# Decoding step of two layers: where the last 64 rows of w3 and wq lie in SBUF

## The chip, the cores and the metric

The kernel runs on one core of a Trainium2 chip. A core has five engines with instruction streams of their own: TensorE (PE; its weight loads are shown as PEld), VectorE (DVE), ScalarE (ACT), GpSimd (POOL) and SyncE (SP). Sixteen DMA engines move data between memory (HBM) and SBUF, which has 128 partitions. The metric is the device time of one execution in microseconds; lower is better.

## The reference

Two layers, each an attention block over a long cache and a mixer block, for one token of two sequences (D = 576, 32 heads, 16384 cached keys of 128, F = 4608).

```python
def _A_ref(x, k_cache, v_cache, wq, wo):
    q = (x @ wq).reshape(B, Sq, H, Dh).transpose(0, 2, 1, 3)
    scores = jnp.einsum("bhqd,bhkd->bhqk", q, k_cache) * (Dh ** -0.5)
    p = _softmax(scores, axis=-1)
    o = jnp.einsum("bhqk,bhkd->bhqd", p, v_cache)
    return o.transpose(0, 2, 1, 3).reshape(B, Sq, H * Dh) @ wo

def _B_ref(x, w1, w2, w3, w4):
    h = _gelu(_layernorm(x, axis=-1) @ w1)
    ...
    x1 = x + hs
    h2 = _gelu(_layernorm(x1, axis=-1) @ w3) @ w4
    return x1 + h2

x = x + _A_ref(_layernorm(x, axis=-1), A_k_cache, A_v_cache, A_wq, A_wo)
x = x + _B_ref(_layernorm(x, axis=-1), B_w1, B_w2, B_w3, B_w4)
```

The last two lines run twice, with the same weights and the same cache. With one token per sequence the four shifted parts of the mixer are zero, so `hs` is a constant. Both layers read the whole K and V caches, 64 tiles of 4 MB each (32 heads of 2 sequences), and all of wq, wo, w3 and w4.

## The kernel before

**Stages.** A layer is `q_projection`, `attention`, `rows_projection` of wo, `z_projection` (w3), GELU, and `rows_projection` of w4; `layer` (L645) lists them. The kernel records every operation in a graph (`Graph`), which puts semaphores between engines; the order of the recording is the order on each engine.

**Memory.** All cache tiles and weights go through one buffer `mem` of six slots of 32 KB a partition (`TILE`). `Store` hands it out: `plan` (L278) queues transfers in a fixed order, `pump` (L286) issues the first of the queue as soon as its place is free, and stops at the first that is not; `release` gives a place back when PE has read it and pumps again. All transfers are issued by SP, in the order of the queue. A plan entry has a list of starts, each a DMA of its own.

**The seam between the layers.** At the end of layer 0's attention two cache tiles stay in their slots for layer 1, and the K chunks of a third are kept. Between them lies a ring of six places of 4608 bytes a partition: four in slot 4 (`a`) and two in slot 1 (`c`), in the turn of L522. wo, w3 and w4 of layer 0 and wq of layer 1 go through it, place after place; `halves` (L525) cuts each block of 128 rows of w3 or wq into two halves of the columns. Behind them come the four quarters of a parked V tile (places 1, 2, 3 and 0 of `a`) and the first quarter of the first fresh K tile (in `c`), in the order of L539; then whole tiles again. In the seam PE also transposes K chunks of the kept tiles (`turn`, L1060) between the weights' matmuls.

**The end.** In layer 1 the weights lie in slots that the last tiles have left: wo in three pieces, w3 as whole blocks of 128 rows with all columns, w4 in six pieces, then w1. L550 to L557 give their places.

**The tail.** D = 576 is four blocks of 128 rows and a tail of 64. In `x` and its normalised form `xn` the 64 tail features lie on partitions 64 to 127 of the fifth block (`TL` = 64). Before, `plan_cols` (L440) loads a tail of w3 or wq with one DMA that splits each row into two halves, so that row r lies on partitions 2r and 2r + 1 and all 128 partitions are filled. To match, `spread_tail` (L719) multiplies the tail features with two selection matrices `sel`, and copies the result as `xt`: two column pairs, each with the features on every second partition and zeros between. `cols_tail` (L759) then needs half as many matmuls as there are column blocks, each with four columns: one pair for the first half of the columns, one for the second. `cols_chunk` (L740) does the full blocks, with one matmul for each 128 columns.

Of the kernel before, what the change touches and what calls it, by code (L numbers as in the profile page):

```python
# [328 lines left out]
class KB:  # L329
# [11 lines left out]
    PARKED = 5  # L341
    GONE = 72
    RAW = 2
    TURNS = {("w3", 0): 1, ("w3", 1): 1, ("w3", 2): 1, ("w4", 1): 1, ("w4", 3): 1, ("w4", 6): 1, ("w4", 8): 1,
             ("wq", 0): 1, ("wq", 1): 1, ("wq", 2): 1}

# [25 lines left out]
    def _alloc(self):  # L372
# [20 lines left out]
        self.spread = self.prod[:, 10 * U:14 * U]  # L393
        self.otn = self.prod[:, 14 * U:15 * U]
        self.fold = sb("fold", [128, 32], BF16)
        self.gT = self.prod[:, 4 * MT * B:5 * MT * B]
        self.z = self.prod[:, 512:512 + 2 * MT * B].bitcast(FP32)
        self.rows = self.prod[:, 1024:1024 + self.D]
# [41 lines left out]
    def plan_cols(self, nm, l, w, parts):  # L440

        self.parts[nm, l] = parts
        for i, (k, m, z, at) in enumerate(parts):
            n = 128 * (z - m)
            if k < self.KT - 1:
                src = w[k * 128:(k + 1) * 128, 128 * m:128 * z]
            else:
                n //= 2
                src = w[k * 128:, :].rearrange("r (h n) -> (r h) n", h=2)
            self.store.plan((nm, l, i), f"{nm}{k}_{m}", at, 2 * n, [(lambda b: b, src)])  # L450

    def whole(self, w, ats):

# [45 lines left out]
    def plan_all(self):  # L499
# [12 lines left out]
        for (t, u), slot in zip(tiles, place):  # L512
# [9 lines left out]
        turn = iter([*a, c[0]] + [a[0], a[1], c[1], a[2], a[3], c[0]] * 6)  # L522
        h = MT // 2
        self.cuts["wo", 0] = [(i, i + 4, next(turn)) for i in range(0, 32, 4)]
        halves = lambda n: [(k, m, z, next(turn)) for k in range(self.KT - 1) for m, z in ((0, n), (n, 2 * n))] + \  # L525
                           [(self.KT - 1, 0, 2 * n, next(turn))]
        w3 = halves(h)
        self.groups = [(0, 4, 8, 12, 16, 18), (0, 8, 12, 16, 18)]
        g = self.groups[0]
# [6 lines left out]
        b, hh = third % self.B, third // self.B  # L536
        tiles = self.tile_order(1)
        b2, h2 = tiles[0][1] % self.B, tiles[0][1] // self.B
        for i in (1, 2, 3, None, 0):  # L539
            if i is None:  # L540
                self.plan_piece(*tiles[0], T, self.K[b2, h2].rearrange("(p j) d -> p (j d)", p=128), 0, quarter)
            else:
                self.plan_piece("v", third, 4 * T, self.V[b, hh].rearrange("(p j) d -> p (j d)", p=128),
                                i * self.GONE // 4, self.GONE // 4)
        place = [(3, 4, 5, 0, 2, 1)[i % 6] for i in range(len(tiles))]
        for i, (t, u) in enumerate(tiles):
            if (t, u) != ("v", third):
                self.plan_tile(t, u, place[i], (quarter, half, half + quarter) if i == 0 else
                               (half,) if i == len(tiles) - 1 else (), 0 if i else quarter)
        self.cuts["wo", 1] = [(0, 11, 2 * T), (11, 22, 2 * T + 11 * row), (22, 32, 0)]  # L550
        at = 10 * row
        w4_at = T + 2 * w3r + w3r // 2
        self.cuts["w4", 1] = [(0, 8, w4_at)] + \
                             [(a, b, 3 * T + (a - 8) * row) for a, b in ((8, 16), (16, 26), (26, 30), (30, 34), (34, 36))]
        self.plan_rows("wo", 1, self.wo, self.cuts["wo", 1])
        self.plan_cols("w3", 1, self.w3, self.whole(self.w3, [at, at + w3r, T, T + w3r, T + 2 * w3r]))
# [88 lines left out]
    def layer(self, l):  # L645
        if l == 0:
            self.unscaled()
        self.q_projection(l)
        if l == 0:
            self.hs_projection()  # L650
            self.quads()
        self.attention(l)
        ot = self.otn.rearrange("p (b j) -> p j b", b=self.B)
        self.rows_projection("wo", l, lambda k: ot[:, k, :], "prod")
        self.add_psum(self.x, "x", self.x, "x", self.unscaled)
        self.layernorm("x", self.x, self.xb, "xb")
        self.dv(lambda e: e.tensor_copy(out=self.mean0[:, :], in_=self.mv[:, 0, :]), reads=["mv"], writes=["mean0"])
        self.dv(lambda e: e.tensor_copy(out=self.rstd0[:, :], in_=self.rstd[:, :]), reads=["rstd"], writes=["rstd0"])
        self.dv(lambda e: e.tensor_tensor(out=self.x1[:, :, :], in0=self.xb[:, :, :], in1=self.hs[:, :, :],
                                          op=ALU.add), reads=["xb", "hs"], writes=["x1"])  # L660
        self.z_projection(l)
        if l == 0:
            self.turn(2, settle=False)
        self.gelu_z()
        self.settle()
        self.rows_projection("w4", l, lambda k: self.gT[:, k * self.B:(k + 1) * self.B], "prod")
        self.dv(lambda e: e.tensor_tensor(out=self.x[:, :, :], in0=self.x[:, :, :], in1=self.x1[:, :, :],
                                          op=ALU.add), reads=["x", "x1"], writes=["x"])
        if l < self.NL - 1:
            self.add_psum(self.x, "x", self.x, "x", self.unscaled)  # L670
        else:
            self.add_psum(self.xo, "xo", self.x, "x")


    def quads(self):

# [39 lines left out]
                                          in1=self.rstd[TL:, :], op=ALU.mult),  # L716
                reads=["tmp1", "rstd"], writes=[dk])

    def spread_tail(self):  # L719

        B, KT = self.B, self.KT

        def f(pe):
            for h in range(2):
# [15 lines left out]
    def cols_chunk(self, w, l, k, out, pk, n, rhs, rk, cols, first, last=False, held=False):  # L740
# [15 lines left out]
        if l == (1 if w == "wq" else 0):  # L756
            self.turn(self.TURNS.get((w, k), 0), settle=not held)

    def cols_tail(self, w, l, out, pk, n, cols):  # L759

        B, k = self.B, self.KT - 1
        nm = (w, l, len(self.parts[w, l]) - 1)
        buf = self.store.buf(nm)

# [29 lines left out]
    def q_projection(self, l):  # L794
# [13 lines left out]
        for k in range(1, KT - 1):  # L808
            self.cols_chunk("wq", l, k, out, [pk], n, self.xn[:, k, :], "xn", cols, k == 1)
            if k == 1:  # L810
                self.spread_tail()
        self.cols_tail("wq", l, out, [pk], n, cols)
        self.act(lambda e: e.activation(out=self.junk[:, :], in_=self.eps[:, :], func=ACT.Exp),
                 reads=["eps"], writes=["junk"])
# [71 lines left out]
    def z_projection(self, l):  # L886
# [8 lines left out]
        self.layernorm("x1", self.x1, self.xn, "xn", after=lambda: chunk(1))  # L895
        if l == 0:
            self.settle()
        self.spread_tail()
        al, be = self.coef[:, 0, :], self.coef[:, 1, :]
        self.dv(lambda e: e.tensor_tensor(out=be, in0=self.mean0[:, :], in1=self.rstd0[:, :], op=ALU.mult),  # L900
                reads=["mean0", "rstd0"], writes=["coef"])
# [555 lines left out]
```

## Time and profile before

| what | value |
|---|---|
| median of 3 runs | 2550.74 us (2550.16 to 2550.76) |
| the profiled execution's own time | 2549.84 us |
| its span, first to last instruction | 2548.1 us |
| bytes moved | 1093.19 MB, mean 429 GB/s over the span |
| busy share PE, DVE, ACT | 63%, 74%, 47% |
| mean granted TensorE clock | 0.574 |

A core's profile is read in this order: the busy shares say which engine could bound the span; the row of slices says where in time the rates change; the chain of waits, followed back from the last instruction, says what ended last at each step. A share is an average over stages with different limits, so the stage around the change is read by itself. In tables by stretches a DMA share can be a little over 1, where packets of an engine overlap. The profile numbers no DMA engine.

### The profile page before, as it was taken

The page shows a single profiled execution, that of the slowest core. Times are in us where ns is not written, and L with a number is a line of the kernel's source. Part 1 is how long each engine was busy: PE and PEld are TensorE (multiplying, and loading weights), DVE is VectorE, ACT ScalarE, POOL GpSimd, SP SyncE. Part 2 cuts the span into 40 slices and gives each one's busy share as a digit, 9 for nine tenths or more (in the row PEclk, how much of TensorE's full clock was granted, in tenths as well). Part 3 has the DMA queues.
Part 4 walks back from the last instruction along what each step waited for, and adds up shares of the span by engine and source line. Part 5 has one row for each costly group of instructions (what it writes and reads, how often), then busy time and mean ns, then how long its engine had stood idle before and what let it go on. Part 6 is the DMA issues. An engine that isn't in the chain of part 4 may idle for free.

```text
span 2548.1 us, 74893 instructions
## 1 busy us (share of the span) xinstructions
PE 1614.7 (63%) x34407; PEld 1580.7 (62%) x34407; DVE 1897.0 (74%) x2062; ACT 1204.2 (47%) x1810; POOL 53.5 (2%) x151
## 2 busy tenths in 40 slices
PE   4666666656666666666777766656665666666566
PEld 3666666656666665666667666656665665666566
DVE  5877777777777777777648877777777777777774
ACT  3544544444454444445435544444454444445442
POOL 0000000000000000000000000000000000000000
PEclk8555555555555555555656555565555555555555
DMA  9999999999999999999999999999999999999999
GB/s 410 428 433 431 432 432 431 433 431 433 430 432 432 432 432 431 433 431 432 419 411 427 432 431 432 432 432 432 432 432 432 432 432 432 432 433 431 433 431 386
DMA packets 46928, 1093.19 MB, mean 429 GB/s; under 512 B 5140, under 2 KB 6296, under 8 KB 12440
## 3 DMA queue, kind: packets, MB, share of 16 engines
q1 hardware_dynamic: 46872, 1092.40, 100.0%
q8 instruction: 41, 0.67, 0.1%
q14 instruction: 15, 0.12, 0.0%
HBM read 1092.37 MB, written 0.00 MB: 429 GB/s over the span
## 4 chain that ended last, share of the span: by engine, by line
DMA 66%; DVE 23%; PE 5%; issue 5%; SPq 1%; ACT 0%; DVEq 0%; POOLq 0%
DMA mem<-in_A_k_cache_dram 63%; DVE s_dve L1291 12%; DVE prod L1287 9%; PE tps L1241 2%; PE mps L1361 2%; DMA mem<-in_B_w_dram 1%; DMA mem<-in_A_wo_dram 1%; PE sps L1267 1%; SPq L101 1%; PE sps L1212 1%; DVE diag L1208 0%; DVE l L1339 0%; DVE q_col L1205 0%; DMA mem<-in_A_wq_dram 0%; DVE mx L1302 0%
## 5 line engine op out<-in xcount | busy, mean ns | idle before, releaser
L1253 ACT ACTIVATE kt<-tps 128x1024 bf16<-128x1024 bf16 x992 | 1002.9, 1023 | 878.0 <-PE tps L1241 859.5
L1291 DVE TENSOR_REDUCE s_dve<-prod 128x16 f32<-128x2048 bf16 x504 | 1152.1, 2286 | 17.3
L1241 PE MATMUL tps<-ident,mem 128*128 128x128 bf16 x8192 | 1000.0, 300 | 141.3 <-POOLq L202 135.2
L1287 DVE TENSOR_TENSOR prod<-mem,qb 128x2048 bf16<-128x2048 bf16 x504 | 616.8, 1224 | 525.4 <-POOLq L202 493.9
L1361 PE MATMUL mps<-p,mem 128*128 128x1 bf16 x16384 | 512.2, 166 | 549.7 <-POOLq L202 519.3
L1241 PEld LDWEIGHTS tps<-ident,mem 128*128 128x128 bf16 x8192 | 761.3, 136 | 151.1 <-POOLq L202 145.0
L1361 PEld LDWEIGHTS mps<-p,mem 128*128 128x128 bf16 x16384 | 487.5, 104 | 558.3 <-ACT p L1322 552.2
L1267 PEld LDWEIGHTS sps<-q_col,kt 128*128 128x128 bf16 x7936 | 399.5, 113 | 0.8 <-ACT kt L1253 0.4
L1267 PE MATMUL sps<-q_col,kt 128*128 128x1 bf16 x7936 | 388.1, 170 | 0.4 <-issue 0.3
L1212 PE MATMUL sps<-diag,ones_bf 128*128 128x128 bf16 x127 | 36.5, 287 | 195.4 <-DVE diag L1208 195.4
L1212 PEld LDWEIGHTS sps<-diag,ones_bf 128*128 128x128 bf16 x127 | 13.2, 104 | 205.6 <-DVE diag L1208 205.6
L1316 ACT ACTIVATE mx<-mx 128x1 f32<-128x1 f32 x128 | 26.0, 203 | 236.2 <-POOL mx L1307 236.2
L1307 POOL PARTITION_ALL_REDUCE mx<-mx x128 | 51.1, 400 | 2441.9 <-DVE mx L1305 2323.7
L1215 ACT ACTIVATE qb<-sps 128x128 bf16<-128x128 f32 x127 | 35.2, 277 | 137.3 <-PE sps L1212 137.3
L1319 ACT ACTIVATE p<-s_dve,mx 128x64 bf16<-128x64 f32 x126 | 43.8, 348 | 4.1
L1253 ACT ACTIVATE mem<-tps 128x1024 bf16<-128x1024 bf16 x32 | 32.0, 1025 | 22.0 <-PE tps L1241 19.6
L1322 ACT ACTIVATE p<-sps,mx 128x64 bf16<-128x64 f32 x128 | 37.7, 294 | 0.1
L1302 DVE TENSOR_REDUCE mx<-sps 128x1 f32<-128x64 f32 x128 | 27.6, 216 | 7.5 <-PE sps L1267 7.5
L874 PE MATMUL mps<-prod,mem 128*128 128x2 bf16 x680 | 22.1, 166 | 14.5 <-DMA mem<-in_B_w_dram 8.8
L1208 DVE TENSOR_SCALAR diag<-ident,q_f 128x128 bf16<-128x128 bf16 x127 | 31.1, 245 | 0.0
L874 PEld LDWEIGHTS mps<-prod,mem 128*128 128x128 bf16 x680 | 20.6, 105 | 16.2 <-DMA mem<-in_B_w_dram 7.5
L707 ACT ACTIVATE misc<-misc 128x2 f32<-128x2 f32 x8 | 2.4, 296 | 51.4 <-DVE misc L705 51.4
(117 smaller groups left out, 293.4 us busy)
## 6 DMA issues: line engine op xcount, KB each, us to landing
mem<-in_A_k_cache_dram SPq DMA_DIRECT2D x124, 4096.0 KB, 40.7
mem<-in_A_v_cache_dram SPq DMA_DIRECT2D x123, 4096.0 KB, 49.6
mem<-in_B_w_dram SPq DMA_DIRECT2D x21, 576.0 KB, 7.7
mem<-in_B_w_dram SPq DMA_DIRECT2D x7, 1152.0 KB, 33.9
mem<-in_A_v_cache_dram SPq DMA_DIRECT2D x3, 2048.0 KB, 40.4
mem<-in_A_wq_dram SPq DMA_DIRECT2D x10, 512.0 KB, 6.5
mem<-in_A_wo_dram SPq DMA_DIRECT2D x8, 576.0 KB, 19.3
mem<-in_A_wq_dram SPq DMA_DIRECT2D x4, 1024.0 KB, 8.0
```

The lines of the kernel that those rows point to most:

```text
L874: ins = pe.matmul(self.mps[:, t * B:(t + 1) * B], lhsT=buf[:, o:o + 128], rhs=rhs(k), start=(k == 0 and t == 0), stop=(k == last), skip_gr ...
L1212: self.pe(lambda pe: pe.matmul(qps, lhsT=self.ones_bf[:, :], rhs=self.diag[:, :], start=True, stop=True, skip_group_check=True), reads=["o ...
L1215: self.act(lambda e: e.activation(out=self.qb[i][:, :], in_=qps, func=ACT.Copy), reads=[("qps", i)], writes=[("qb", i)], sig=("qb", i))
L1241: ins = pe.transpose(self.tps[t][:, j * 128:(j + 1) * 128], buf[:, j * 128:(j + 1) * 128], self.ident[:, :])
L1253: self.act(lambda e: e.activation(out=out, in_=self.tps[t][:, :], func=ACT.Copy), reads=[("tps", t)], writes=keys, sig=("evac", c, t, k))
L1267: ins = pe.matmul(self.sps[sp][:, c * self.CH + j:c * self.CH + j + 1], lhsT=buf[:, j * 128:(j + 1) * 128], rhs=self.q_col[:, sp:sp + 1], ...
L1287: self.dv(lambda e: e.tensor_tensor(out=prod, in0=buf.rearrange("p (j d) -> p j d", d=128), in1=qbc, op=ALU.mult), reads=[("qb", r)] + key ...
L1291: self.dv(lambda e: e.tensor_reduce(out=sd[:, c0:c0 + DB], in_=prod, axis=AX.X, op=ALU.add), reads=["prod"], writes=[("s_dve", r)], sig=(" ...
L1307: self.pool(lambda e: e.partition_all_reduce(mx[3], mx[2], channels=128, reduce_op=ROP.max), reads=[("mx2", i)], writes=[("mx3", i)])
L1319: self.act(lambda e: e.activation(out=p[:, n:self.NB], in_=self.s_dve[i][:, 0:self.NB - n], func=ACT.Exp, bias=mx[4], scale=self.scale, ac ...
L1322: self.act(lambda e: e.activation(out=p[:, 0:n], in_=self.sps[i][:, 0:n], func=ACT.Exp, bias=mx[4], scale=self.scale, accum_out=self.ls[:, ...
L1361: ins = pe.matmul(self.mps[:, 448:449], lhsT=buf[:, j * 128:(j + 1) * 128], rhs=p[:, col:col + 1], start=b == 0, stop=b == self.NB - 1, sk ...
```

## The change

`LOW` names three tails: w3 of both layers and wq of layer 1. Their 64 rows now lie whole on partitions 0 to 63. Each part is loaded by two DMAs of 32 rows; the source is read as `(j i) n -> i j n` with i = 8, so that row 8j + i of the 32 lands on partition 4i + j. In the ring (w3 of layer 0, wq of layer 1) the tail is cut into two halves of the columns like the other blocks, and takes two places instead of one, each with 64 of its 128 partitions filled; in layer 1's w3 it stays one part, of 9216 bytes a partition. wq of layer 0 is loaded as before.

To match, `row_order` writes a 64 x 64 permutation into `diag` (a matrix that attention uses otherwise) after the attention of each layer. `spread_tail` multiplies the tail features with it once, and `xt` has two columns on 64 partitions. `low_tail` takes one matmul of two columns and 64 rows for each column block, and gives back each half's place for itself.

Since the ring is two places longer, the turn ends elsewhere: the parked V tile's quarters come in the order 2, 3, 0, 1, and the K quarter after them. In layer 1, wo is cut 10, 10, 12 instead of 11, 11, 10, w3 lies two rows' width further on, and w4's first piece moves from slot 1 to slot 2.

```diff
+    LOW = (("w3", 0), ("wq", 1), ("w3", 1))
...
+        self.perm = self.diag[:, 0:self.TL]
...
-            if k < self.KT - 1:
-                src = w[k * 128:(k + 1) * 128, 128 * m:128 * z]
-            else:
+            starts = [(lambda b: b, w[k * 128:min((k + 1) * 128, self.D), 128 * m:128 * z])]
+            if k == self.KT - 1 and (nm, l) in self.LOW:
+                starts = [(lambda b, r=r: b[r:r + 32, :],
+                           w[k * 128 + r:k * 128 + r + 32, 128 * m:128 * z].rearrange("(j i) n -> i j n", i=8))
+                          for r in (0, 32)]
+            elif k == self.KT - 1:
                 n //= 2
-                src = w[k * 128:, :].rearrange("r (h n) -> (r h) n", h=2)
-            self.store.plan((nm, l, i), f"{nm}{k}_{m}", at, 2 * n, [(lambda b: b, src)])
+                starts = [(lambda b: b, w[k * 128:, :].rearrange("r (h n) -> (r h) n", h=2))]
+            self.store.plan((nm, l, i), f"{nm}{k}_{m}", at, 2 * n, starts)
...
-        halves = lambda n: [(k, m, z, next(turn)) for k in range(self.KT - 1) for m, z in ((0, n), (n, 2 * n))] + \
-                           [(self.KT - 1, 0, 2 * n, next(turn))]
+        halves = lambda n: [(k, m, z, next(turn)) for k in range(self.KT) for m, z in ((0, n), (n, 2 * n))]
...
-        for i in (1, 2, 3, None, 0):
+        for i in (2, 3, 0, 1, None):
...
-        self.cuts["wo", 1] = [(0, 11, 2 * T), (11, 22, 2 * T + 11 * row), (22, 32, 0)]
-        at = 10 * row
-        w4_at = T + 2 * w3r + w3r // 2
-        self.cuts["w4", 1] = [(0, 8, w4_at)] + \
+        self.cuts["wo", 1] = [(0, 10, 2 * T), (10, 20, 2 * T + 10 * row), (20, 32, 0)]
+        at = 12 * row
+        self.cuts["w4", 1] = [(0, 8, 2 * T + 20 * row)] + \
...
         self.attention(l)
+        if ("w3", l) in self.LOW:
+            self.row_order()
...
+    def row_order(self):
+
+        TL = self.TL
+        for r in (0, 32):
+            self.dv(lambda e, r=r: e.tensor_copy(
+                out=self.perm[TL:, r:r + 32].rearrange("p (i j) -> p i j", i=8),
+                in_=self.ident[TL:, TL + r:TL + r + 32].rearrange("p (j i) -> p i j", i=8)),
+                reads=["ident"], writes=["diag"])
...
-    def spread_tail(self):
-
-        B, KT = self.B, self.KT
+    def spread_tail(self, w, l):
+
+        B, KT, TL = self.B, self.KT, self.TL
+        if (w, l) in self.LOW:
+            t = self.mps[0:TL, 384:384 + B]
+            self.pe(lambda pe: pe.matmul(t, lhsT=self.perm[TL:, :], rhs=self.xn[TL:, KT - 1, :], start=True, stop=True),
+                    reads=["xn", "diag"], writes=["mps"])
+            self.dv(lambda e: e.tensor_copy(out=self.xt[0:TL, 0:B], in_=t), reads=["mps"], writes=["xt"])
+            return
...
+    def low_tail(self, w, l, out, pk, cols):
+
+        B, TL = self.B, self.TL
+        for i, (k, lo, hi, _) in enumerate(self.parts[w, l]):
+            if k < self.KT - 1:
+                continue
+            nm = (w, l, i)
+            buf = self.store.buf(nm)
+
+            def f(pe, buf=buf, lo=lo, hi=hi):
+                for m in range(lo, hi):
+                    ins = pe.matmul(out[:, m * B:(m + 1) * B], lhsT=cols(buf, m, lo)[0:TL, :], rhs=self.xt[0:TL, 0:B],
+                                    start=False, stop=True, skip_group_check=True)
+                return ins
+            self.pe(f, reads=["xt"] + self.store.keys(nm), writes=pk)
+            self.store.release(nm)
+
     def cols_tail(self, w, l, out, pk, n, cols):
 
         B, k = self.B, self.KT - 1
+        if (w, l) in self.LOW:
+            return self.low_tail(w, l, out, pk, cols)
```

More of the change, by code (lines that the diff above doesn't have):

```diff
@@ L810, in q_projection @@
             if k == 1:
-                self.spread_tail()
+                self.spread_tail("wq", l)
         self.cols_tail("wq", l, out, [pk], n, cols)
@@ L897, in z_projection @@
             self.settle()
-        self.spread_tail()
+        self.spread_tail("w3", l)
         al, be = self.coef[:, 0, :], self.coef[:, 1, :]
```

## The prediction

> **What bounds the kernel now.** I read the profile's page first (slices, queues, chain of waits), then a table by stretches of time around the two places where the changed weights are loaded, then the instructions there in order of time.
>
> ```profile
> DMA  9999999999999999999999999999999999999999
> GB/s 410 428 433 431 432 432 431 433 431 433 430 432 432 432 432 431 433 431 432 419 411 427 432 431 432 432 432 432 432 432 432 432 432 432 432 433 431 433 431 386
> ...
> q1 hardware_dynamic: 46872, 1092.40, 100.0%
> q8 instruction: 41, 0.67, 0.1%
> ...
> DMA 66%; DVE 23%; PE 5%; issue 5%; SPq 1%; ACT 0%; DVEq 0%; POOLq 0%
> ```
>
> All 16 DMA engines work from the first slice to the last; the queue that SP feeds takes 100.0% of their time. No engine's instructions bound the span: the bytes do. Rates sag only in slices 19 to 21 (the seam between the layers) and 39 (the end). The question there is whether engines wait or only move small pieces, which the table by stretches answers (stretch; its length; busy time and count of PE, weight loads, VectorE, ScalarE, GpSimd; clock; DMA share; GB/s):
>
> ```profile
> 1210.00:1230.00 20.00, 12.88 (x267) 12.75 (x268) 15.51 (x16) 9.82 (x16) 0.35 (x1) 0.57 1.00 433
> ...
> 1290.00:1295.00 5.00, 4.71 (x103) 4.56 (x102) 0.56 (x4) 3.90 (x4) 0.00 (x0) 0.50 1.03 411
> ...
> 1310.00:1315.00 5.00, 2.67 (x70) 2.39 (x68) 0.61 (x4) 2.51 (x3) 0.00 (x0) 0.50 0.99 369
> ...
> 2535.00:2540.00 5.00, 2.07 (x58) 1.90 (x55) 0.92 (x7) 0.73 (x2) 0.00 (x0) 0.50 1.01 402
> 2540.00:2541.00 1.00, 0.04 (x1) 0.04 (x2) 0.30 (x2) 0.84 (x1) 0.00 (x0) 0.50 0.93 346
> 2541.00:2542.00 1.00, 1.00 (x39) 1.00 (x40) 0.00 (x0) 0.00 (x0) 0.00 (x0) 0.50 0.74 289
> 2542.00:2543.00 1.00, 1.00 (x38) 0.95 (x34) 0.00 (x0) 0.00 (x0) 0.00 (x0) 0.50 0.60 230
> 2543.00:2544.00 1.00, 0.32 (x13) 0.29 (x12) 0.00 (x0) 0.00 (x0) 0.00 (x0) 0.50 0.53 190
> 2544.00:2545.00 1.00, 0.81 (x26) 0.66 (x22) 0.15 (x1) 0.00 (x0) 0.00 (x0) 0.50 0.49 164
> 2545.00:2546.00 1.00, 0.74 (x8) 0.46 (x9) 0.17 (x2) 0.00 (x0) 0.00 (x0) 0.50 0.06 22
> ```
>
> Even in the seam the share is 0.99 to 1.03: no engine waits for work worth a term. At the end the share does not drop at once. It falls from 0.93 to 0.53 between 2540 and 2544, stays near 0.5, and goes to 0.06 after 2545. So about half of the engines have run out by 2543.5, and the other half go on for up to 2.5 us. The engines are not in step, and the last weights are there when the late half is done. PE then follows at once:
>
> ```profile
> 2520.94 22.72 DMA mem<-in_B_w_dram
> 2543.66 0.05 issue
> 2543.71 1.12 PE mps L874 x30
> ```
>
> That piece of the chain of waits (start, length, what) is w4's last large piece, landing at 2543.66. Hence the rule for the sum: the time is the load of the most loaded DMA engine, plus a fixed rest behind the last w4 piece. A transfer is worth what it adds to the engines that are late.
>
> **The change, part by part.** *The three tails.* Bytes stay the same: 576 KB for each w3 tail, 512 KB for wq's. Before, 128 partitions spread them over 16 engines. After, the source's slowest dimension is 8, and the change says eight engines. At 433 GB/s an engine moves 433/16 = 27.1 GB/s. A w3 tail on 16 engines is 36,864 B each, 1.36 us; on eight it is 73,728 B, 2.72 us. So the loaded eight get +1.36 us and the others -1.36. wq's tail is 1.21 us before and 2.42 after: +1.21 and -1.21. Over the run: 1.36 + 1.21 + 1.36 = 3.9 us more on eight engines, as much less on the other eight. With the share at 1.00 there is no idle time in which the loaded eight could hide it, and static shares of every later transfer never even it out.
>
> [...] No row here numbers the engines.
>
> *Seven more transfers* (4 for 1, 4 for 1, 2 for 1). What one more transfer costs is not isolated in the trace. From above: the whole seam (1260 to 1330), small transfers, instruction fetches and all, ran at this rate.
>
> ```profile
> DMA packets 6454, 28.40 MB, mean 406 GB/s; under 512 B 720, under 2 KB 720, under 8 KB 5827
> ...
> mem<-in_A_wq_dram SPq DMA_DIRECT2D x9, 512.0 KB, 6.5
> ...
> mem<-in_A_k_cache_dram SPq DMA_DIRECT2D x4, 1024.0 KB, 8.8
> ```
>
> 576 KB take 1.45 us at 406 GB/s against 1.36 at 433, so at most 0.09 us each, 0.6 for seven. From below: 0, or less, since the same bytes move in rows no shorter than before. I take 0.1, because the fetches explain part of the lower rate. The sum on the loaded eight is 4.0 us.
>
> *Which engines are late.* The half that ends after 2545 need not be the loaded half. But it is enough that one of the late eight is among the loaded eight: that one then ends about 4.0 us later. All late engines end within the one us from 2545 to 2546, so the last of such an overlap was at most 1 us before the very last. I take 0.4 off: **+3.6 us**. If all eight late ones are the relieved ones, the first rival applies.
>
> *Two ring places a tail, the ring shifted by one, then two.* Each half place is a full place of time on the loaded engines, so they see the same pace. 512 KB land 6.5 us after issue for 1.21 us of transfer: about 5.3 us of lead for the slow engines. The relieved eight lose 2.6 us of queued work over the two tails in the seam and may run dry there, which costs nothing while they are ahead. SP issues seven more DMAs, each about this long:
>
> ```profile
> 1296.05 11.13 SPq L101 DMA_DIRECT2D mem<-in_A_wq_dram  x9
> ...
> 1312.61 0.33 SPq L101 DMA_DIRECT2D mem<-in_A_k_cache_dram  x1
> ```
>
> That is 7 x 0.33 = 2.3 us of SP, four of them per 2.5 to 2.8 us of transfer, inside that lead: nothing. The K quarter moves behind all four quarters of the parked V tile. It was issued at 1312.61 and lands 8.8 us later, near 1321.4; with 2.6 us of tails and one 576 KB piece more it lands near 1325.4. PE first transposes a fresh chunk of that tile at 1328.96, and PE moves 2.6 us too: 0.
>
> ```profile
> 1328.96 0.88 PE tps L1241 x8
> ```
>
> *PE and VectorE.* These rows (start, length, engine, line, operation, idle before and its releaser) are layer 0's tail and layer 1's:
>
> ```profile
> 1287.09 0.74 PE L751 MATMUL sps<-xn,mem 128*128 128x2 bf16 x18 [0.66 <-DMA mem<-in_B_w_dram]
> ...
> 1288.61 0.72 PE L768 MATMUL sps<-xt,mem 128*128 128x4 bf16 x18 [0.78 <-DMA mem<-in_B_w_dram]
> ```
> ```profile
> 2518.46 1.49 PE L874 MATMUL mps<-prod,mem 128*128 128x2 bf16 x50 [0.72 <-DMA mem<-in_A_wo_dram]
> 2519.99 0.16 DVE L852 TENSOR_TENSOR x<-x,mps 128x8 f32<-128x8 f32 x1 [6.17 <-PE mps L874]
> ...
> 2526.67 0.16 DVE L729 CAST xt<-mps 128x4 bf16<-128x4 f32 x1 [0.31 <-PE mps L725]
> ...
> 2529.61 1.78 PE L751 MATMUL sps<-xn,mem 128*128 128x2 bf16 x36 [1.00 <-DMA mem<-in_B_w_dram]
> ...
> 2531.41 0.96 PE L768 MATMUL sps<-xt,mem 128*128 128x4 bf16 x18
> ...
> 2532.67 0.26 ACT L917 ACTIVATE prod<-prod 128x72 bf16<-128x72 f32 x1 [5.61 <-DVE prod L913]
> ...
> 2534.20 1.20 PE L874 MATMUL mps<-prod,mem 128*128 128x2 bf16 x40 [1.83 <-DMA mem<-in_B_w_dram]
> ```
>
> In layer 0 the tail becomes 18 + 18 matmuls of two columns. The first 18 run while the second half is still in transfer; behind the last landing stand 18 as before (0.74 against 0.72): 0. wq's 16 + 16 go the same way. In layer 1 36 matmuls follow one landing: 1.78 for 0.96, +0.82. GELU would end at 2532.93 + 0.82 = 2533.75, still ahead of 2534.20, where PE waited for w4's first piece; tail and piece slip together. Without that cover it would cost 0.82. The two copies of the row order are priced by the cast (0.16 each) and run while VectorE sits idle before L852, 6.17 us in layer 1 and more in layer 0: 0. One matmul for two before the tail: a gain of 0.1 off the path. wo's last piece in layer 1 has 12 rows for 10, 60 matmuls for 50, +0.3; the wait of 1.00 for w3's fourth piece swallows it.
>
> The sum is made against the profiled execution, span 2548.1, time 2549.84: 2553.4. The median of the runs shown is 0.9 above that execution, so **2554.3 us**.
>
> **The rivals.**
> *The late eight are just the relieved eight.* For it: late and early engines are eight and eight, so a split by halves is possible. Against it: one engine of overlap breaks it, and no row names them. The late ones then end 4.0 earlier, near 2541.5; the early ones, out by 2543.5, end by 2547.5, 1.5 past the old 2546: 2552.2. 18%.
> *The same, and the seam forgets.* If in addition the relieved eight waited in the seam for ring places until both halves were in step, only layer 1's tail would count: 2543.5 + 1.4 and 2546 - 1.4 both end near 2544.8, a gain of 1.2: 2549.5. Perfect balance would gain the mean idle share before 2546, 0.07 + 0.26 + 0.40 + 0.47 + 0.51 + 0.94 = 2.65 us, so no balancing reaches 0.2%. Against: shares of 0.99 and more leave nothing to forget with. 3%.
> *The split does not happen.* Sixteen engines after all, no term left: 2550.7. Against it the source's dimension of 8. 5%.
> *The ring runs dry* (the slower side). If a half-filled place is released so late that the loaded engines lose their lead, one full lead is paid: 5.3 us on top of 3.6, 2559.6. It decides from the point where a place's turnaround exceeds six places of transfer, 6 x 1.36 = 8.2 us, against 6.5 now. For it: the share at 1310 to 1315 is the lowest of the seam. Against: each half is consumed sooner than the whole was. 12%.
>
> [...]
>
> **How the numbers follow.** Forecast 62%, rivals 18, 3, 5 and 12. Its own range is 2553 to 2555.5 (0.4 left out or 1 us taken off; 0 to 0.6 for the transfers). To leave out no more than 2 in 10 the range takes in the first and third rival, and a part of a stall: 2550.5 to 2557. A measurement of this kernel tells about 0.2%, 5.1 us, from no change. The forecast and the first three rivals lie inside, less 3% for stalls that begin small: same 0.85, slower 0.13, faster 0.02.
>
> **What would show it.** Right: the DMA share stays near 1.0 through the seam, and at the end the plateau with half of the engines busy is longer than 2.5 us, about 4 to 8, with w4's last pieces landing 3 to 4 us later. The first rival: a plateau of another length with the end only 1 to 2 us later. A dry ring: shares clearly below 1 in the seam, with PE waiting for w4 or wq there. PE exposed: L874's wait for w4's first piece gone. I am wrong if the time falls by a us or more, or rises by over 5.

## The result and the profile after

| | before | after |
|---|---|---|
| median | 2550.27 us (2549.35 to 2551.47, 22 runs) | 2553.30 us (2552.54 to 2555.14, 22 runs) |
| span of the profiled execution | 2548.1 us | 2550.8 us |
| ratio | | 1.0013, 95% interval 1.0007 to 1.0019 |

The changed kernel is 3.0 us slower (2553.30 - 2550.27), between 1.8 and 4.8 us by the interval. The forecast was 2554.3.

The page of the kernel after, the rows that answer to those of before (slices, queues, shares of the chain of waits):

```profile
DMA  9999999999999999999999999999999999999999
GB/s 409 429 431 432 432 432 432 432 432 432 432 432 432 431 432 432 433 431 433 417 399 428 430 432 431 433 432 431 433 431 434 429 434 429 434 429 434 429 434 380
...
q1 hardware_dynamic: 46840, 1092.40, 99.9%
...
DMA 65%; DVE 24%; PE 5%; issue 5%; SPq 1%; ACT 0%; DVEq 0%; POOLq 0%; POOL 0%
```

Transfers still bound the span, with the same 1092.40 MB. The split over eight engines is read from the semaphores: each transfer of 32 rows makes nine updates, one 0.4 us after its issue ends (in the seam about 1.1 us after it starts) and eight as it lands, where a transfer to 128 partitions makes sixteen. The slices that lost are those of the seam (419 and 411 GB/s became 417 and 399) and the last (386 became 380). The table by stretches shows what happened in them. First one row of the kernel before that was not shown above (columns as there):

```profile
1285.00:1290.00 5.00, 3.57 (x72) 3.38 (x69) 1.29 (x8) 2.57 (x3) 0.00 (x0) 0.50 1.02 409
```

And the kernel after:

```profile
1285.00:1290.00 5.00, 4.09 (x94) 3.85 (x93) 1.26 (x6) 2.31 (x2) 0.00 (x0) 0.50 0.93 326
...
1310.00:1315.00 5.00, 3.16 (x72) 2.72 (x72) 0.40 (x2) 2.70 (x4) 0.00 (x0) 0.50 0.88 328
...
2540.00:2541.00 1.00, 0.91 (x34) 0.92 (x35) 0.00 (x0) 0.00 (x0) 0.00 (x0) 0.50 1.07 420
2541.00:2542.00 1.00, 0.74 (x14) 0.65 (x11) 0.18 (x2) 0.00 (x0) 0.00 (x0) 0.50 0.89 358
2542.00:2543.00 1.00, 0.00 (x0) 0.00 (x0) 0.65 (x5) 0.62 (x2) 0.00 (x0) 0.50 0.88 335
2543.00:2544.00 1.00, 0.38 (x14) 0.39 (x15) 0.39 (x3) 0.96 (x1) 0.00 (x0) 0.50 0.92 353
2544.00:2545.00 1.00, 1.00 (x42) 1.00 (x39) 0.00 (x0) 0.00 (x0) 0.00 (x0) 0.50 0.70 262
2545.00:2546.00 1.00, 0.70 (x25) 0.61 (x21) 0.00 (x0) 0.00 (x0) 0.00 (x0) 0.50 0.44 159
2546.00:2547.00 1.00, 0.60 (x20) 0.60 (x20) 0.00 (x0) 0.00 (x0) 0.00 (x0) 0.50 0.30 102
2547.00:2548.00 1.00, 0.52 (x14) 0.35 (x11) 0.32 (x2) 0.00 (x0) 0.00 (x0) 0.50 0.14 48
```

Two things are new. At each tail of the seam the DMA share falls: from 1.02 to 0.93 at w3's, from 0.99 to 0.88 at wq's. That is (0.09 + 0.11) x 5 us x 16 = 16 engine-us, 2.0 us for each of the eight relieved engines: by that reading they ran out of work and gave back most of the 2.57 us by which they had been relieved (no row names the engines that stand idle). At w3's tail the rate fell more than the share (326 / 0.93 = 351 GB/s while busy, against 409 / 1.02 = 401), so there the packets themselves also took longer (those of 4608 bytes 208 ns in the mean, 181 before). At the end the level near one half that stood before from 2543 to 2545 (0.53, 0.49, then 0.06) is gone. The share now runs down step by step.

The chain of waits places the loss in time (start, length, what). The first row is the stream's last K tile, the second a large piece of w4; the kernel before, then the kernel after:

```profile
2447.17 40.72 DMA mem<-in_A_k_cache_dram
```
```profile
2450.00 40.72 DMA mem<-in_A_k_cache_dram
...
2523.29 23.06 DMA mem<-in_B_w_dram
```

The last K tile lands at 2450.00 + 40.72 = 2490.72 instead of 2487.89, 2.83 us later: that is the seam with its two tails. w4's last large piece lands at 2546.35 instead of 2543.66, 2.69 us later. So in this execution layer 1's tail, which lies between the two, shows no cost (55.63 us from the one landing to the other, 55.77 before; how far that distance scatters is told below). From that piece to the end of the span it is 4.45 us, against 4.44 before.

PE in layer 1's end, in order of time (start, length, engine, line, operation, idle before and its releaser):

```profile
2532.49 1.77 PE L771 MATMUL sps<-xn,mem 128*128 128x2 bf16 x36 [1.01 <-DMA mem<-in_B_w_dram]
2534.53 1.75 PE L790 MATMUL sps<-xt,mem 64*128 64x2 bf16 x36 [0.28 <-DMA mem<-in_B_w_dram]
...
2537.34 1.21 PE L913 MATMUL mps<-prod,mem 128*128 128x2 bf16 x40 [1.06 <-DMA mem<-in_B_w_dram]
...
2546.40 1.16 PE L913 MATMUL mps<-prod,mem 128*128 128x2 bf16 x30 [0.70 <-DMA mem<-in_B_w_dram]
```

The tail's 36 matmuls take 1.75 us behind their landing, and PE still waits 1.06 us for w4's first piece and 0.70 for the last one shown. The longer tail of PE is covered.

### The profile page after: what moved, and what is told of

It is laid out like the page before. It is cut to its first block, busy times and chain, and to the rows that moved or that the text cites. A ratio compares the mean times of both kernels' runs of the same rounds, so it can differ in the third digit from the quotient of the medians.

```text
span 2550.8 us, 75002 instructions
## 1 busy us (share of the span) xinstructions
PE 1616.1 (63%) x34456; PEld 1581.6 (62%) x34456; DVE 1897.8 (74%) x2066; ACT 1204.6 (47%) x1810; POOL 53.5 (2%) x151
## 3 DMA queue, kind: packets, MB, share of 16 engines
q1 hardware_dynamic: 46840, 1092.40, 99.9%
## 4 chain that ended last, share of the span: by engine, by line
DMA 65%; DVE 24%; PE 5%; issue 5%; SPq 1%; ACT 0%; DVEq 0%; POOLq 0%; POOL 0%
DMA mem<-in_A_k_cache_dram 63%; DVE s_dve L1330 13%; DVE prod L1326 9%; PE tps L1280 2%; PE mps L1400 2%; DMA mem<-in_B_w_dram 1%; SPq L101 1%; PE sps L1306 1%; PE sps L1251 1%; DVE diag L1247 0%; DMA mem<-in_A_wo_dram 0%; DVE l L1378 0%; DVE mx L1341 0%; DVE q_col L1244 0%; DVE mx L1339 0%
## 5 line engine op out<-in xcount | busy, mean ns | idle before, releaser
L1339 DVE TENSOR_REDUCE mx<-s_dve 128x1 f32<-128x64 f32 x126 | 26.3, 209 | 0.0
```

## The experiments

Each is the changed kernel with the edit shown. Differences in us are medians against the kernel before, which ran beside them: 2550.16 for e1 to e4, 2550.33 for e6 to e9, 2550.06 for e10 and e11. One such ratio is known to about 0.09% (2.3 us) either way, 0.14% (3.5 us) for e3, e4, e8 and e10, so where less is at stake I go by two landings in the profiled execution: the last K tile's and that of w4's last large piece. These are worked out from the increments of the transfers' semaphores, which the trace records, and agree with the chain's rows where it has them. The profiled executions of e3 and e8 took 2563.29 and 2563.37 us, 2.8 and 1.8 above their medians, so their landings add up to more than the last column.

| run | last K tile | against before | w4's piece | distance | median against before |
|---|---|---|---|---|---|
| before | 2487.89 | | 2543.66 | 55.77 | |
| e1_seam_tails | 2490.60 | +2.71 | 2546.32 | 55.72 | +2.5 |
| e6_w3_seam | 2489.25 | +1.36 | 2546.04 | 56.79 | +2.7 |
| e7_wq_seam | 2489.70 | +1.81 | 2545.66 | 55.96 | +2.0 |
| e2_layer1_tail | 2488.22 | +0.33 | 2544.69 | 56.47 | +0.9 |
| after | 2490.72 | +2.83 | 2546.35 | 55.63 | +3.0 |
| e11_changed_again | 2491.07 | +3.18 | 2547.55 | 56.48 | +3.3 |
| e9_half_again | 2490.78 | +2.89 | 2548.62 | 57.84 | +5.2 |
| e3_sixteen_engines | 2496.24 | +8.35 | 2557.19 | 60.95 | +10.3 |
| e8_sixty_four_rows | 2496.37 | +8.48 | 2556.74 | 60.37 | +11.3 |
| e10_one_transfer | 2494.04 | +6.15 | 2555.28 | 61.24 | +11.8 |
| e4_four_engines | 2498.62 | +10.73 | 2563.59 | 64.97 | +20.1 |

e1, e6 and e7 leave layer 1's tail as it was, and their distances are 55.72, 56.79 and 55.96. So a distance scatters by about 1 us between executions, and a smaller difference between two of them says nothing by itself. Likewise e2 has no tail of the seam and shows +0.33 there.

**The two tails of the seam alone.**

```diff
-    LOW = (("w3", 0), ("wq", 1), ("w3", 1))
+    LOW = (("w3", 0), ("wq", 1))
```

> The two tails of the seam (w3 of layer 0, wq of layer 1) on eight engines; layer 1's w3 tail on 128 partitions and 16 engines again, in the changed kernel's places. If the load of the slowest DMA engine sets the time and the seam's two tails are paid in full while layer 1's costs almost nothing (in the changed kernel's trace the last landing of the stream is 2.8 us later than before, and that of w4 2.7): +2.5 to +3.2 us over the kernel before, the same as the whole change. If each tail adds its own share (1.36, 1.21 and 1.36 less 0.4): +2.4 here, and the whole change 1 us more.

Measured: 2552.64 us, ratio 1.001 (1.0001 to 1.0019), +2.5 us. The chain of this run has the last K tile at 2449.84 + 40.76 = 2490.60:

```profile
2449.84 40.76 DMA mem<-in_A_k_cache_dram
...
2524.06 22.26 DMA mem<-in_B_w_dram
```

The seam's two tails carry most of the loss. The median fits both theories of the expectation (2.5 to 3.2, and 2.4). The sum for the loaded engines was 1.36 + 1.21 = 2.57 us, and the stream as a whole is late by about that. The sixteen increments of the V half tile behind that K tile show it: the first came 2.6 us later than before, the last 2.7 us, and put in order of time the sixteen are 1.7 to 3.2 us later, 2.5 in the mean. None is earlier, so a gain of the relieved half does not show there.

**Each of the two by itself.** With the other tail, and layer 1's, laid out as in the kernel before:

```diff
-    LOW = (("w3", 0), ("wq", 1), ("w3", 1))
+    LOW = (("w3", 0),)
...
+        last = lambda n: [(k, m, z, next(turn)) for k in range(self.KT - 1) for m, z in ((0, n), (n, 2 * n))] + \
+                         [(self.KT - 1, 0, 2 * n, next(turn))]
...
-        self.plan_cols("wq", 1, self.wq, halves(H // 2))
+        self.plan_cols("wq", 1, self.wq, last(H // 2))
```

> Layer 0's w3 tail alone goes to eight engines; wq's tail and layer 1's stay as in the kernel before. Load theory: each tail of the seam adds its own length on eight engines, and the ring makes all sixteen wait for them: 576 KB at 433 GB/s, +1.4 us over the kernel before (1.0 to 1.8). Rival: the seam pays one disturbance, whatever its size (a ring place released late): then this tail alone costs the 2.5 us of both, or nothing.

The second of the pair has `LOW = (("wq", 1),)` and `w3 = last(h)`.

> Layer 1's wq tail alone goes to eight engines; both w3 tails stay as in the kernel before. Load theory: +1.2 us over the kernel before (0.8 to 1.6), and with the run of w3's tail alone it makes up the +2.5 us of both. Rival of one disturbance: +2.5 us or 0.

Measured: 2553.05 us (ratio 1.0013, 1.0004 to 1.0022) and 2552.30 us (1.0008, 0.9999 to 1.0017), +2.7 and +2.0. Both medians lie above the ranges of the load theory (1.0 to 1.8 and 0.8 to 1.6) and nearer to the rival's 2.5, but their intervals exclude neither. The last K tile moves by +1.36 and +1.81; together 3.2, against 2.7 and 2.8 where both tails are changed. So by the landings each tail costs by itself, and it isn't one disturbance paid once; w3's agrees with its 1.36, wq's is 0.6 above its 1.21. e6's median lies above its landing; in its profiled execution the distance too was the longest of the three with an unchanged layer 1, and why is not shown. The DMA share falls where the changed tail is, and only there; the first two rows are e6's, the other two e7's:

```profile
1285.00:1290.00 5.00, 4.00 (x92) 3.80 (x90) 1.13 (x6) 2.31 (x2) 0.00 (x0) 0.50 0.86 279
1310.00:1315.00 5.00, 2.91 (x74) 2.62 (x71) 0.77 (x4) 3.23 (x4) 0.00 (x0) 0.50 1.03 411
```
```profile
1285.00:1290.00 5.00, 3.61 (x72) 3.42 (x70) 1.40 (x8) 2.57 (x3) 0.00 (x0) 0.50 1.01 404
1310.00:1315.00 5.00, 2.52 (x67) 2.26 (x66) 0.00 (x0) 2.51 (x3) 0.00 (x0) 0.50 0.92 325
```

What no run separates is the load from the other things that a changed tail brings into the seam: a half-filled place more in the ring, and three more transfers. For the load speak the sizes (1.36 for 1.36, and 2.7 to 2.8 for 2.57; but 1.81 for 1.21). So in the seam the cause is argued and not isolated.

**Layer 1's tail alone.** The seam as in the kernel before:

```diff
-    LOW = (("w3", 0), ("wq", 1), ("w3", 1))
+    LOW = (("w3", 1),)
...
-        halves = lambda n: [(k, m, z, next(turn)) for k in range(self.KT) for m, z in ((0, n), (n, 2 * n))]
+        halves = lambda n: [(k, m, z, next(turn)) for k in range(self.KT - 1) for m, z in ((0, n), (n, 2 * n))] + \
+                           [(self.KT - 1, 0, 2 * n, next(turn))]
...
-        for i in (2, 3, 0, 1, None):
+        for i in (1, 2, 3, None, 0):
```

> Only layer 1's w3 tail on eight engines; the seam as before, with one place a tail and the old order of the quarters. If that tail's load falls on engines that are not the last ones: between -0.5 and +0.6 us. If each tail adds its own share: +1.0 to +1.4 us. In both cases half of the engines get 1.36 us earlier at the end, and the last of the loaded ones 1.36 us later.

Measured: 2551.06 us, ratio 1.0004 (0.9995 to 1.0013), +0.9 us: between the two theories, so the time doesn't settle it. The table by stretches at its end:

```profile
2543.00:2544.00 1.00, 1.00 (x36) 0.93 (x33) 0.00 (x0) 0.00 (x0) 0.00 (x0) 0.50 0.72 255
2544.00:2545.00 1.00, 0.28 (x11) 0.27 (x11) 0.00 (x0) 0.00 (x0) 0.00 (x0) 0.50 0.26 91
2545.00:2546.00 1.00, 0.85 (x27) 0.69 (x23) 0.09 (x1) 0.00 (x0) 0.00 (x0) 0.50 0.14 48
2546.00:2547.00 1.00, 0.68 (x6) 0.40 (x7) 0.23 (x2) 0.00 (x0) 0.00 (x0) 0.50 0.07 24
```

The same second without the change had 0.53 and then 0.49 with half of the engines at work. Here 0.72 are busy to 2544, then 0.26, 0.14 and 0.07: most engines end together, and about two in sixteen go on past 2545 (0.14 x 16). That is what comes out if most of the late engines are relieved ones and most of the early ones loaded ones, with a few loaded engines that were late already. The sixteen increments of w4's last large piece say the same: before, eight come from 2538.28 to 2541.23 and eight from 2542.48 to 2543.66; here two come at 2537.40 and 2537.51, twelve from 2540.22 to 2542.72, and two at 2544.53 and 2544.69. With 0.33 us for the later K tile and 1.36 either way for the tail, the two earliest of before would come at 2537.25 and 2537.54 if they were relieved, and a late one at 2544.17 or later if it was loaded. So two of the late eight are loaded ones, by this estimate; no row names them.

**The changed kernel once more.**

> The changed kernel once more, for a second profiled execution of it: +2.5 to +3.5 us over the kernel before. In the first one layer 1's tail cost nothing at the end (w4's last large piece came 55.6 us after the stream's last K tile, 55.8 in the kernel before). If the tail's load is hidden by engines that were early, this distance again lies between 55.4 and 56.5; if it costs its full 1.36 us and the first was chance, it is 57 or more.

Measured: 2553.32 us, ratio 1.0013 (1.0004 to 1.0022), +3.3 us, distance 56.48. Its chain:

```profile
2450.34 40.73 DMA mem<-in_A_k_cache_dram
2524.48 23.07 DMA mem<-in_B_w_dram
```

The distance lies at the edge of the range said for a hidden load (55.4 to 56.5). Against the one execution of before (55.77), layer 1's tail cost -0.14 us in the first execution of the changed kernel and +0.71 in this one, +0.70 with the seam undone; the mean of these three distances, 56.19, is 0.13 above the mean of the four with an unchanged layer 1, 56.06. With a scatter of 1 us that says less than the full 1.36, and not much more. By the medians it is 0.9 (alone) and 0.5 (3.0 less 2.5).

**Half of layer 1's tail loaded twice.** The second copy (288 KB) lies where nobody reads it, and only adds load to eight engines, as the tail itself does:

```diff
+            at3 = (self.TILE + 6 * self.F) // 2
+            more = [(lambda m, r=r: self.store.mem[r:r + 32, at3:at3 + self.F // 2],
+                     self.w3[512 + r:544 + r, :self.F // 2].rearrange("(j i) n -> i j n", i=8))
+                    for r in (0, 32)] if (l, i) == (1, 0) else []
-            self.store.plan((nm, l, i), f"{nm}{i}", at, 2 * (b - a) * D, [
+            self.store.plan((nm, l, i), f"{nm}{i}", at, 2 * (b - a) * D, more + [
```

> The changed kernel, and ahead of w4's first piece in layer 1 one half of w3's tail (288 KB) is loaded a second time, by two more 32-row transfers on the same eight engines, to a place that nobody reads. Theory that the most loaded engine sets the end: 288 KB are 1.36 us on each of eight engines, and the changed kernel left these last, so all of it shows: +1.36 us over the changed kernel, +4.4 us over the kernel before (3.9 to 4.8). Rival, the bytes alone count: 288 KB at 433 GB/s, +0.68 us, +3.7 us over the kernel before. Rival, the other eight engines are still the last at the end: +0 to +0.4 us, +3.0 to +3.4 us over the kernel before.

Measured: 2555.53 us, ratio 1.0021 (1.0012 to 1.003), +5.2 us. The chain:

```profile
2450.04 40.74 DMA mem<-in_A_k_cache_dram
...
2526.61 22.01 DMA mem<-in_B_w_dram
```

w4's piece lands at 2548.62, 57.84 us behind the K tile: 1.4 and 2.2 us more than in the two executions of the changed kernel. The median is above the 3.9 to 4.8 said, and its interval (3.1 to 7.7 us over the kernel before) holds all three theories. The landings favour the load: 1.4 and 2.2 us for 1.36 said. One distance scatters by 1 us, but the sixteen increments of that piece tell the rivals apart. The first seven come from 2539.40 to 2543.14, where the two executions of the changed kernel had 2539.40 to 2542.82 and 2539.42 to 2543.49; the last eight come from 2544.83 to 2548.62, where they had 2543.60 to 2546.35 and 2543.94 to 2547.55. So nearly half of the engines did not move, and the later half moved by 0.9 to 2.3 us at these ends. Had the bytes counted for everybody, all would have moved by 0.68. So the slack of the loaded engines at the end is used up by the first copy.

**Sixteen engines for each 32 rows.**

```diff
-                           w[k * 128 + r:k * 128 + r + 32, 128 * m:128 * z].rearrange("(j i) n -> i j n", i=8))
+                           w[k * 128 + r:k * 128 + r + 32, 128 * m:128 * z].rearrange("(j i) n -> i j n", i=1))
```

(and i = 1 in `row_order`).

> The whole change, but the 32 rows of each transfer are read in their own order, so that a transfer is split over 16 engines with two partitions each. Ring places, seven more transfers, matmuls and row order stay. If the load of engines is the cause: within 0.5 us of the kernel before. If the half-filled places, the transfers or the longer ring are the cause: +2.5 to +3.5 as in the whole change. If two engines that write to neighbouring partitions hinder each other so that 32 partitions take twice the time on all 16 engines: +3.9 us or more, because then all 16 engines pay 1.36 + 1.21 + 1.36.

Measured: 2560.5 us, ratio 1.004 (1.0026 to 1.0054), +10.3 us. Neither the time of even load nor the +2.5 to +3.5 of places and transfers; only the third theory (+3.9 or more) allows for it. The stretches of w3's tail in the seam:

```profile
1285.00:1290.00 5.00, 1.94 (x36) 1.58 (x34) 1.02 (x5) 2.31 (x2) 0.00 (x0) 0.50 1.04 201
1290.00:1295.00 5.00, 2.18 (x55) 2.04 (x56) 0.00 (x0) 0.00 (x0) 0.00 (x0) 0.50 1.00 318
```

All engines are busy (1.04) and move 201 GB/s where the kernel before moved 409: the packets take twice as long (those of 4608 bytes 375 ns in the mean of the first stretch, 181 before).

**Four engines** (i = 4 in the same places).

> The whole change with a slowest source dimension of 4: each transfer of 32 rows on four engines. A tail then costs each of the four 5.45 us (w3) or 4.84 us (wq) where 16 engines take 1.36 and 1.21: +4.09 and +3.63 in the seam, +4.09 in layer 1. If engine load is the cause: +7.7 us for the seam's two, plus 0 to 4.1 for layer 1's, +7.7 to +11.8 in all, less what these four engines are ahead of the last one (up to 3 us). If places, transfers and matmuls are the cause: +3 as before.

Measured: 2570.25 us, ratio 1.0082 (1.0069 to 1.0096), +20.1 us, more than the load on four engines gives:

```profile
1285.00:1290.00 5.00, 2.29 (x48) 2.09 (x45) 0.91 (x4) 2.31 (x2) 0.00 (x0) 0.50 0.93 243
1290.00:1295.00 5.00, 0.93 (x24) 0.88 (x25) 0.00 (x0) 0.00 (x0) 0.00 (x0) 0.50 1.01 285
```

Here too the second row has all engines busy at 285 GB/s. By load alone the twelve other engines would have gone on at full rate until they ran out of work.

**64 rows in one transfer on sixteen engines.** To see whether 32 rows were too few or partitions 0 to 63 the reason:

```diff
-                starts = [(lambda b, r=r: b[r:r + 32, :],
-                           w[k * 128 + r:k * 128 + r + 32, 128 * m:128 * z].rearrange("(j i) n -> i j n", i=8))
-                          for r in (0, 32)]
+                starts = [(lambda b: b[:64, :], w[k * 128:, 128 * m:128 * z])]
```

> Each tail is the 64 rows in their own order on partitions 0 to 63, by one transfer (two in the seam, one for each half of the columns) on sixteen engines: half as many transfers as with sixteen engines and 32 rows each, which cost +10.3 us over the kernel before. If what costs is that sixteen engines write into partitions 0 to 63 only, the tails again move at about 200 GB/s with the engines busy, and the time is +8 to +12 us. If what cost was 32 rows to a transfer, or the number of transfers, sixteen engines share the tail evenly again and the time is +0 to +1.5 us. The load theory by itself, which counts bytes for each engine and not where they are written, says +0 to +0.6 us.

Measured: 2561.6 us, ratio 1.0044 (1.003 to 1.0058), +11.3 us, as with 32 rows and within the +8 to +12 of the first theory:

```profile
1285.00:1290.00 5.00, 1.86 (x33) 1.51 (x32) 0.92 (x4) 2.31 (x2) 0.00 (x0) 0.50 1.02 185
1290.00:1295.00 5.00, 2.18 (x55) 2.03 (x53) 0.18 (x2) 0.00 (x0) 0.00 (x0) 0.50 1.00 320
```

The number of rows and of transfers isn't it. The packets are of the same 4608 bytes as before, and take 402 ns in the mean of the first stretch. What is left is where the rows are written. Half of the 409 GB/s of before would be 205, and the traces are near it, with 185 here and 201 with 32 rows. Why partitions 0 to 63 take about half of the rate with sixteen engines at work, no run shows.

**One transfer of 64 rows on eight engines.** Eight engines again, as in the changed kernel, but row 8j + i now lies on partition 8i + j:

```diff
-                starts = [(lambda b, r=r: b[r:r + 32, :],
-                           w[k * 128 + r:k * 128 + r + 32, 128 * m:128 * z].rearrange("(j i) n -> i j n", i=8))
-                          for r in (0, 32)]
+                starts = [(lambda b: b[:64, :], w[k * 128:, 128 * m:128 * z].rearrange("(j i) n -> i j n", i=8))]
```

(and `row_order` permutes the 64 at once).

> Each tail (each half of its columns in the seam) is one transfer of 64 rows on the same eight engines, in place of two of 32: engine by engine the same bytes, but an engine now fills eight neighbouring partitions, 8i to 8i + 7, where the changed kernel gave it 4i to 4i + 3 and 32 + 4i to 35 + 4i. Load theory, in which only the number of engines counts: as the changed kernel, +3.0 us over the kernel before, or a little less for five transfers fewer (2.5 to 3.3). Theory that two engines must not write the same group of partitions at one time (by the runs with sixteen engines on partitions 0 to 63, which moved about 200 GB/s with the engines busy): packets get longer with eight engines too, and the time is +5 to +12 us over the kernel before.

Measured: 2561.85 us, ratio 1.0047 (1.0033 to 1.006), +11.8 us:

```profile
1285.00:1290.00 5.00, 2.58 (x51) 2.14 (x49) 1.01 (x5) 2.31 (x2) 0.00 (x0) 0.50 0.94 245
```

It still goes to eight engines: the tail's second half, issued at 1282.81, makes one update of its semaphore at 1283.84 and eight from 1289.64 to 1292.26 (the first half's eight come from 1287.36 to 1289.90). The share of 0.94 is that of the changed kernel (0.93), but the rate is 245 GB/s instead of 326. The theory that only the number of engines counts falls. What differs from the changed kernel is the order of the rows over the partitions, and one transfer in place of two: if each engine takes one i, it fills 4i to 4i + 3 of each 32 partitions there, and eight neighbouring ones here. The times are +3.0 and +11.8 us. That the partitions an engine writes are the reason is an inference: no row says which engine wrote which.

The size of the loss is accounted for only in part. By load and packet time, sixteen engines with packets twice as long add about 3.9 us, as the three tails take 3.9 us on sixteen engines. Eight engines with packets of about 0.28 us (eight packets in the 2.2 us from the first half's increments to the second's) add about 8, and four engines 7.7 to 11.8. Measured were 10.3 and 11.3, 11.8, and 20.1. The packets' own records show where part of the rest lies. With four engines, 265 packets of 4608 bytes start between 1287.5 and 1292.5; all but three take more than 230 ns, 306 in the mean, against 181 before. Together they fill 81 us, all that sixteen engines have in these 5 us. So packets of other transfers are slowed as well (the tail's two halves, 64 rows each, have 128 in all), and no sum by load or by the tail's own packets contains that. Why they are slowed was not tried.

None of these versions beats the kernel before.

## Why the prediction was right, and where not

*The most loaded engine sets the time, and a fixed rest follows.* Right. The rest is 4.45 us against 4.44 (4.4 to 4.8 in all runs), and a load put on eight engines alone shows in full at the end (e9: the landing 1.4 and 2.2 us later, for 1.36). The sum takes all three tails to fall on the same eight engines; no row shows that, and what e9 showed fits it: the later eight increments moved by 0.9 to 2.3 us at their ends, the first seven by less than 0.4 either way.

*Three tails, 1.36 + 1.21 + 1.36.* Right for the seam: 2.57 was said, 2.71 (e1) and 2.83 (after) were measured. Too much for layer 1's: its share was 1.36 less 0.4 for the engines' being out of step, about 1.0; the medians give 0.5 to 0.9, and the landings 0.1 in the mean. The sum of 3.6 became 2.7 in the first execution and 3.0 in the medians. The mis-sized term is the one for *which engines are late*: taken as 0.4, it was 0.5 to 0.9 by the medians and 1.2 by the mean of the landings. The step itself, that one loaded engine among the late ones is enough, fits e2: by the estimate there two of the late eight were loaded, and the last of them came 0.7 us later against the K tile, 1.36 less 0.7. That the other late engines were relieved ones is argued from the same increments; to that extent the first rival holds at the end.

*Seven more transfers, 0.1.* Not isolated. The seam has six of the seven, and its delay less the load is 0.1, 0.3 and 0.6 us (2.71, 2.83 and 3.18 less 2.57), with the executions' scatter in it: no sign of more than 0.1 each. SP's part was mis-sized. The prediction took 0.33 us an issue from a transfer on sixteen engines; a tail's 32-row issue in the seam takes 0.67 to 0.78, as in these four for wq's tail:

```profile
1307.82 2.83 SPq L101 DMA_DIRECT2D mem<-in_A_wq_dram  x4
```

At w3's tail four of them run back to back from 1282.18 to 1285.12. Behind them w4's first piece is issued at 1285.16 (1282.43 before): in the longer ring it takes the place of w3's fifth half block instead of the fourth, which PE had read at 1284.43, and the rest is SP's. Both can keep work from the relieved eight; what each costs by itself no run shows.

*The ring.* "Which costs nothing while they are ahead" was wrong in its consequence. By the fall of the DMA share (to 0.93 and 0.88) the relieved eight did run dry, and it was not the running dry that cost, but their relief was gone with it: at the last transfer through the ring (the K quarter; a V quarter before, behind the same bytes) the first increment is already 2.1 us later than before (1322.04 against 1319.97) and the last 2.0 (1323.99 against 1321.95), and at the V half tile late in layer 1 the sixteen are 1.1 to 2.8 us later (1.7 to 3.2 in e1), none earlier. Hence the seam's tails cost their full load whichever engines are late at the end, and the overlap that the prediction argued over matters only for layer 1's tail. The second rival ("the seam forgets", 2549.5) had this the wrong way: what is forgotten is the gain of the relieved half, not the loss of the loaded one. The fourth rival's full lead of 5.3 us on top was not paid: the last K tile is late by the tails' load alone.

*PE and VectorE, 0.* Right: 1.75 us for the tail's matmuls (1.78 said), a wait of 1.06 left of 1.83 (1.83 less the 0.82 of the prediction is 1.01), and behind wo's longer piece a wait of 1.01 for w3's fourth piece is still there.

*The signs named beforehand.* w4's last pieces 2.7 us later, just under the 3 to 4 named. The share near 1.0 through the seam: wrong, 0.93 and 0.88. A longer level at one half at the end: wrong, for the two reasons above (the relief was lost in the seam, and layer 1's tail evened the ends out).

*The third rival's price.* "Sixteen engines after all: 2550.7" counted bytes only. With sixteen engines the time is 2560 to 2562 (e3, e8). The case didn't arise; but how the rows are spread over engines and partitions, which the forecast did not ask, weighs up to three times its whole sum (+10.3 to +11.8 us in e3, e8 and e10, against 3.6). That the layout in question does not pay that price was luck, as far as the forecast goes.

## What to carry to other kernels

Where transfers bound the time, cost an edit by the load of each engine, and then ask whether a ring behind it makes the others wait: if so, the transfers on half of the engines cost everybody their extra length here (2.71 and 2.83 us for 2.57), and only behind the last ring place could engines that were early hide part of it (0.5 to 0.9 us by the medians, for 1.36). Before a tile is narrowed to some of the partitions, try its rows in more than one order: the same rows on eight engines cost 3.0 us in one and 11.8 in another (one transfer in place of two went with it, which with sixteen engines made no such difference: 10.3 and 11.3).

## What the runs showed of the hardware that was not expected

The DMA share did not tell a slow engine from a full one here. With sixteen engines on partitions 0 to 63 it was 1.02 to 1.04 at 185 to 201 GB/s, against 1.02 at 409 for the same weights on 128 partitions; only the rate beside it shows that the packets took longer (375 and 402 ns in the mean for 4608 bytes, against 181). And the engines of one transfer were up to 5.4 us out of step by themselves: the sixteen landings of w4's last large piece lie between 2538.28 and 2543.66 in the kernel before, though there every large transfer fills all 128 partitions. 41 packets of instructions, 1.06 us each in the mean, come on top of the weights and tiles; on which engines, and so whether they are part of it, no row says. And in the seam SP took about twice as long to issue 32 rows on eight engines: 0.67 to 0.78 us, against 0.33 to 0.42 on sixteen (e3).
